# SyncE takes over the stores of the result, GpSimd copies the zero-padded half of v on chip, and the order of the steps is replaced

## The chip, the cores and the metric

The kernel runs on one core of one Trainium2 chip. The core has five engines with a queue each: TensorE (PE, with its weight loads PEld), VectorE (DVE), ScalarE (ACT), GpSimd (POOL) and SyncE (SP, which here only issues transfers). The metric is the device time of one execution in microseconds (us); lower is better. The kernel before took 326.9 us (median of three runs, 325.95 to 327.83).

## The reference

The inputs q, k, v, a_re and a_im have 4 batches, 8 heads, 768 steps and 48 columns. For each batch and head a complex state of 48x48 decays from step to step and takes in the outer product of k and v; q reads its real part:

```python
scale = np.minimum(mag, 0.999) / (mag + 1e-06)      # mag = |a|, a = a_re + i a_im
for t in range(S):
    S_re, S_im = ar*S_re - ai*S_im + kv, ar*S_im + ai*S_re
    y[:, :, t] = einsum('bhd,bhde->bhe', q[:, :, t], S_re)
```

The heads of a step are then laid side by side as x (768 rows of 384 columns for each batch). A causal convolution over five steps, column by column, goes through a sigmoid and gives a gate; x @ w_val is multiplied by the gate, and the product by w_out is the result:

```python
gate = 1.0 / (1.0 + np.exp(-gate_pre))
return (gate * (x @ w_val) @ w_out)
```

## The kernel before, in words

**Attention.** The decay is a product of complex numbers, so the kernel takes its logarithm (level) and its angle, sums both up along the steps, and scales k by the inverse of the running product (giving `kx`) and q by the product itself (`qx`). Real and imaginary part lie side by side, 96 columns for a head. Work is cut into nine units (`UNITS`): of batch 0 the first half of the steps in two units of 2 and 6 heads, and then each half of the steps of a batch with all 8 heads. For a unit ScalarE and VectorE compute the scaled q and k (letters `a` to `r` of the order). TensorE transposes them (`T`, line 524), ScalarE copies each transposed tile out of PSUM (`U`, line 532 by the helper at line 150): 128 such copies in all. `kx` also goes to DRAM and back (`K` and `N`), because the state needs it with the steps on the partitions.

A half of the steps has three chunks of 128 steps; with pairs of head rows this gives 51 chunks. For each chunk TensorE makes the scores (`s`), VectorE multiplies them by a triangular mask (`M`), TensorE adds k and v into the state (`t`), ScalarE copies the state out (`u`), TensorE makes the outputs (`y`, lines 626 to 637) and ScalarE copies them out (`v`, into `y_sb`).

**The padded half of v.** A chunk's scores are packed into three blocks of 64 columns, and the first of them belongs to one head on partitions 0 to 63 and to its partner head on partitions 64 to 127. The matmul at line 637 therefore takes its weights from `v_lo`: a copy of v's first 64 steps of each chunk, at partitions 0 to 63 for heads 0 to 3 and at 64 to 127 for heads 4 to 7, with zeros elsewhere. `v_lo` is one buffer for all batches, cleared once (line 278). `load_vl` fills it by two DMAs per unit from DRAM, ten in all, right after the loads of v (`V`); for the next batch they must wait until the last output of the batch before has read it.

**Convolution and projection.** The finished outputs are moved into `xT`, with columns on the partitions, by small DMAs (`X`, 80 issues, on GpSimd's queue). VectorE and ScalarE compute the convolution (`C`, `D`) and the sigmoid (`G`). TensorE multiplies by w_val (`P`, line 719, 24 steps of six matmul instructions) and by w_out (`O`, line 726, 24 steps of six); VectorE multiplies by the gate (`Z`); ScalarE copies a projected block of 128 rows out of PSUM (`Q`) into `ot`, which has two buffers, and the block is stored (`W`, 24 DMAs).

**The guard.** `guard` (`E`, three steps) checks on VectorE that the sums stayed in range, adds up the hits on TensorE (line 507) and writes one integer, `flag` (line 509). After the last step every engine loads the flag (line 821) and branches around a slow fallback (line 937), which is not taken here. Then the program ends with each engine's drain and a barrier among the engines (line 963).

**What sets the order.** `ORDER` is a string of 1119 letters. Each letter runs one step of its stream (`streams`, line 804), and each engine's instructions keep the order in which the steps issue them: `turn` ties every instruction of TensorE, VectorE and ScalarE to the one before. With `PIN_SP = False` the instructions of SyncE and GpSimd are not tied so and the framework places them. `dma` takes its queue from the stream's letter: those in `POOLQ` go to GpSimd's queue, the others to SyncE's. So in the kernel before GpSimd issues `X` and `W`, and SyncE all the loads and `K`.

ScalarE needs another table when it changes between the function sets of `a`, `c`, `f`, `p` (logarithm and exponential), of `o` (sine; `d` may use either this or the next) and of `G` (sigmoid); the order of the steps fixes how many table loads there are.

Of the kernel before, what the change touches and what calls it, by code (L numbers as in the profile page):

```python
# [10 lines left out]
F32 = mybir.dt.float32  # L11
# [16 lines left out]
PIN_SP = False  # L28
POOLQ = 'XW'
TAP0 = 'act'  # L30
ORDER = (
    "AaaabaLwwwwwwAbwwVAcccefgiilmceAAAdhhjdphhkkLjkkqAfgiinproAoqrKnooaalmppNwwbcdcqrTTAATqraKVthehUafuj"
    "bktUcTTUgkceUUisMsiuslnfMdtgwoioThNyilmpUTUmAATUhqMLTTvUUTUTuUpyvTTtqUTsMyutssrTTpuMUUvryUMUtwsvyTpT"
    "AuAaMwvabtTwssUuwcyMvjAkceAktKNyMvTUUUuryvtTfTgwqnUAAAATTiyUUssTTTXMutivoyoqusUTdtUUUlTuUUtTMTXXTXvy"
    "rmXutMaKhThvyaUTUbUsvwMjpXkcUqyvsMcsMkUpTuUNyvTTynVUUvTTeXrXwwXUUsstwTMTTMTsXfgywooutvMyutqCvCyCDDCu"
    "DtUUTUUATUTTTUUUsUvuwTsTPUMysTMCCdthGvuDhUPUDjGArZtyZTaMTTvyaiUUKkNUvTTiUluknssUbcmpCTTPMUyCtCswdMMu"
    "tvTooyAqAPAuCAXUvyqGZOTcQZTteOpUTAUutTrrUTQOvhUTuUXfsgiMisaabyUUvlKsXTTcMyhmjXUcMvykNkWQXpXPPZVvetpn"
    "oToXWqZOUTODDDDutUTUCTCutXQTCUTUsTDsUPCutMDDdsyGCUPMGZDTDWhWQDAZqhvryuvOQGPZrfWWtugAOOUjMQUaakQATUTA"
    "yTUbUTTUTUiUvcissWlMyTkncsUTTUmMvtuKpNATMUqUyvWoPTZTTyUUAeoTTvTsMtufsyMsqKNgtivypuAitUOUTMUTUXrXTvyd"
    "QuthUhjvTuUPUkUssMsyvMlknooWmZPZpyvOQprOQMyvVtuqTUTUTTUUtTrTTUUUTTUTTTUsMUsyTTMqrXXutvuyvtustUUUUuMX"  # L40
    "XTTTXCXKyTUTUssUMMWvyNTsTvyMDUUUDCUtvyuTTTvCUCTTUUstUUsMWTCsMyMutTDTTCCGXDXUTvyutXUTUvyutXUUUssMsMPP"
    "vyMPPZDvyXCOvuXCCyGZPQGZZZWODvXXCDDDPZDGDCQWDDDPDZPCOQWOQOOWQQOECCGZPCDPGDDPZCCOCCCCCCCWQOWQGWOZPQDD"
    "GZGZOWQOOWEEWQWQQWW"
# [9 lines left out]
def kernel(  # L53
# [140 lines left out]
    def load_vl(u):  # L194
        b, h0, g, f0, nf = units[u]
        for w in range(2):
            hs = slice(w * (H // 2) + h0, w * (H // 2) + h0 + g // 2)
            dma(
                "V", out=v_lo[w * HC:(w + 1) * HC, hs].rearrange("i h n e -> i (h n) e"),
                in_=v[b, hs].rearrange("h (n w i) e -> w i (h n) e", w=2, i=HC)[0],  # L200
            )
# [75 lines left out]
    v_lo = const.tile([C, H, NCH, D], F32, name="v_lo")  # L277
    nc.gpsimd.memset(v_lo, 0.0)
# [513 lines left out]
    def v_loads():  # L792
        for u, (b, h0, g, f0, nf) in enumerate(units):
            if f0 == 0:
                load_v(u)
                load_vl(u)
                yield
# [170 lines left out]
```

## Time and profile before

| | us |
|---|---|
| median of three runs | 326.9 |
| profiled execution | 327.57 |
| its span on the core | 325.9 |
| PE busy | 279.0 |
| ACT busy | 241.3 |
| DVE busy | 240.1 |
| POOL busy | 59.6 |

The span goes from the first to the last instruction of one execution; the profiled execution's own time is 1.7 us longer. An engine's busy time is the union of its instructions. Matmuls overlap one another and their ends are modelled, so a busy PE need not be working at its peak. Issuing, waiting, loading the flag and branching are sequencer work (shown as PEq, SPq and so on) and do not count as busy. A row that names a waiting instruction, an arrow and a releaser says what ended the wait, how long the waits were in total, how many there were and the longest of them.

### The profile page before, as it was taken

To read this page: it belongs to the slowest core of one execution; us is meant where nothing else is said; L and a number is where in the kernel's file an instruction comes from. 1 tells how busy PE (TensorE), PEld (TensorE's weight loads), DVE (VectorE), ACT (ScalarE), POOL (GpSimd) and SP (SyncE) were. 2 spreads that over 40 slices of the span, in tenths; PEclk is the share of its full clock that TensorE was granted. 3 is DMA by queue.
4 is the path that set the end of the run, shared out by engine and by line. 5 is a ranking of instruction groups with operands and counts; after the bars stand their busy time and mean duration, and the time that the engine had idled before them with its cause. 6 is when DMAs were issued, how large, how long until landed. Compare 5 with 4: busy or idle time off the path is not lost.

```text
span 325.9 us, 7175 instructions
## 1 busy us (share of the span) xinstructions
PE 279.0 (86%) x2887; PEld 209.5 (64%) x2887; DVE 240.1 (74%) x289; ACT 241.3 (74%) x430; POOL 59.6 (18%) x129
## 2 busy tenths in 40 slices
PE   0341578999998999999999999999999999999960
PEld 0220356888778778677776778777888966555530
DVE  6798899999999899897799956765637436646500
ACT  5999999999998999989985998858477604114310
POOL 6000000032330302033000223304033120321110
PEclk9999999999999999999999999999999999999995
DMA  7997999899999999779994981734555010121120
GB/s 187 270 224 186 296 279 334 266 256 245 253 207 253 314 213 208 241 229 250 183 160 163 277 204 38 261 91 100 110 188 129 3 36 24 39 76 68 71 80 6
DMA packets 84278, 57.18 MB, mean 175 GB/s; under 512 B 40959, under 2 KB 80142, under 8 KB 83342
## 3 DMA queue, kind: packets, MB, share of 16 engines
q1 hardware_dynamic: 80142, 47.21, 59.8%
q0 software_dynamic: 4096, 9.44, 10.7%
q8 instruction: 25, 0.41, 0.6%
q14 instruction: 15, 0.12, 0.1%
HBM read 37.76 MB, written 14.16 MB: 159 GB/s over the span
## 4 chain that ended last, share of the span: by engine, by line
PE 51%; ACT 17%; issue 11%; DMA 9%; DVE 4%; POOL 3%; SPq 1%; POOLq 0%; ACTq 0%
PE mm L719 10%; PE mm L524 8%; PE mm L726 7%; PE S_ps L591 6%; PE y_ps L626 5%; PE sc_ps L553 5%; DMA v_lo<-in_v_dram 4%; ACT tmp L147 4%; PE mm L361 2%; PE y_ps L636 2%; PE y_ps L631 2%; ACT lv L147 2%; ACT kT L150 2%; POOL out_dram L157 2%; PE sc_ps L555 2%
## 5 line engine op out<-in xcount | busy, mean ns | idle before, releaser
L157 POOL DMA_DIRECT2D xT<-y_sb x80 | 41.0, 519 | 72.5 <-ACT y_sb L150 72.3
L688 DVE SCALAR_TENSOR_TENSOR z<-xT,cw_sb,z 128x768 f32<-128x768 f32 (+1 forms) x60 | 50.2, 854 | 5.2 <-ACT z L147 4.3
L719 PE MATMUL mm<-xT,w_sb 128*128 128x384 f32 x144 | 50.2, 493 | 0.0
L726 PE MATMUL mm<-w_sb,z 128*128 128x384 f32 x144 | 49.6, 491 | 0.0
L569 DVE TENSOR_TENSOR sm<-sc_ps,mask 128x384 f32<-128x384 f32 (+1 forms) x51 | 26.8, 530 | 29.4 <-PE sc_ps L558 21.2
L591 PE MATMUL S_ps<-v_in,kn 128*96 128x48 f32 x320 | 35.6, 252 | 7.4 <-DMA kn<-kd 6.2
L591 PEld LDWEIGHTS S_ps<-v_in,kn 128*96 128x96 f32 x320 | 32.4, 168 | 13.4 <-DMA kn<-kd 6.0
L150 ACT COPY y_sb<-y_ps 112x256 f32<-112x256 f32 (+1 forms) x51 | 19.0, 373 | 29.1 <-PE y_ps L636 29.1
L726 PEld LDWEIGHTS mm<-w_sb,z 128*128 128x128 f32 x144 | 26.5, 190 | 17.0 <-ACT kT L150 0.5
L553 PE MATMUL sc_ps<-qT,kT 96*64 96x128 f32 x192 | 36.6, 287 | 0.6 <-DVE sm L569 0.6
L554 PE MATMUL sc_ps<-qT,kT 96*64 96x128 f32 x192 | 36.7, 287 | 0.5 <-ACT qT L150 0.5
L719 PEld LDWEIGHTS mm<-xT,w_sb 128*128 128x128 f32 x144 | 26.4, 190 | 16.6
L145 ACT ACT_TABLE_LOAD x25 | 32.1, 1283 | 1.2 <-PEq L952 0.8
L157 POOL DMA_DIRECT2D out_dram<-ot x24 | 13.2, 550 | 104.4 <-ACT ot L150 86.8
L524 PE MATMUL mm<-ident,kx 128*96 128x128 f32 x192 | 30.0, 286 | 1.5 <-DVE lv L441 0.7
L150 ACT COPY kT<-mm 96x384 f32<-96x384 f32 x64 | 28.6, 486 | 0.5 <-PE sc_ps L558 0.2
L150 ACT COPY ot<-mm 128x384 f32<-128x384 f32 x24 | 11.4, 474 | 23.6 <-PE mm L726 13.1
L150 ACT COPY qT<-mm 96x384 f32<-96x384 f32 x64 | 28.2, 492 | 0.8 <-PE mm L524 0.7
L524 PE MATMUL mm<-ident,qx 128*96 128x128 f32 x192 | 28.3, 280 | 0.2 <-DVE cw_sb L331 0.2
L555 PE MATMUL sc_ps<-qT,kT 96*64 96x64 f32 x192 | 27.3, 224 | 0.0
L558 PE MATMUL sc_ps<-qT,kT 96*64 96x64 f32 x192 | 27.1, 223 | 0.0
L743 DVE TENSOR_TENSOR z<-mm,z 128x384 f32<-128x384 f32 x24 | 13.0, 554 | 15.6 <-ACT z L147 9.4
(90 smaller groups left out, 586.5 us busy)
## 6 DMA issues: line engine op xcount, KB each, us to landing
kd<-kx SPq DMA_DIRECT2D x7, 1152.0 KB, 5.6
out_dram<-ot POOLq DMA_DIRECT2D x24, 192.0 KB, 2.2
ar_in<-in_a_re_dram SPq DMA_DIRECT2D x7, 576.0 KB, 8.9
ai_in<-in_a_im_dram SPq DMA_DIRECT2D x7, 576.0 KB, 9.7
k_in<-in_k_dram SPq DMA_DIRECT2D x7, 576.0 KB, 6.5
q_in<-in_q_dram SPq DMA_DIRECT2D x7, 576.0 KB, 7.8
kn<-kd SPq DMA_DIRECT2D x7, 576.0 KB, 4.4
kn<-kd SPq DMA_DIRECT2D x14, 288.0 KB, 6.3
```

Of the source, the lines that this page charges most:

```text
L145: turn("act", nc.scalar.preload_act_table_set(sets[0]))
L150: return turn("act", nc.scalar.copy(out, in_))
L157: ins = (nc.gpsimd if pool else nc.sync).dma_start(**kw)
L524: pe(nc.tensor.transpose(pt[:C2, j, :], src[:, j, f, h, :], ident))
L553: pe(nc.tensor.matmul(lo[:, :C], part(u, 0, ha, n, 0, HC), part(u, 1, ha, n), start=True, stop=True))
L554: pe(nc.tensor.matmul(hi[:, 0::2], part(u, 0, hb, n, 0, HC), qb, start=True, stop=True))
L555: pe(nc.tensor.matmul(lo[:, C:], part(u, 0, hb, n, HC, C), part(u, 1, hb, n, HC, C), start=True, stop=True))
L558: pe(nc.tensor.matmul(hi[:, 1], part(u, 0, ha, n, HC, C), part(u, 1, ha, n, HC, C), start=True, stop=True))
L591: pe(nc.tensor.matmul(S_ps[bank(u, rs)][:C2, (2 * (h0 + r) + w) * D:(2 * (h0 + r) + w + 1) * D], kn[:, at:at + C2], v_b[b][:, head(u, h), ...
L688: dve(nc.vector.scalar_tensor_tensor(out=z, in0=xT[:, c, EXT + t0 - t:EXT + t0 - t + n], scalar=cw_sb[:, TAPS - 1 - t, c:c + 1], in1=z, op ...
L719: pe(nc.tensor.matmul(pv[:, :n], wv_sb[:, ci, c * P:(c + 1) * P], xT[:, ci, EXT + t0:EXT + t0 + n], start=(ci == 0), stop=(ci == NT - 1),))
L726: pe(nc.tensor.matmul(po[:, :DM], z[:, ci, m:m + P], wo_sb[:, ci, :], start=(ci == 0), stop=(ci == NT - 1)))
```

## The change

Five edits. `POOLQ` loses `W`, so SyncE issues the 24 stores of the result. `PIN_SP` is true, so SyncE's and GpSimd's instructions keep the order of the steps too. `load_vl` and its ten DMAs go; a new stream `B`, with one step per unit, copies the same part of v from `v_in` to `v_lo` on GpSimd, two copies per unit. `v_lo` is now two buffers, one for each half of the steps. `ORDER` is a new string of 1128 letters, in which the guard's steps stand further ahead of the end.

```diff
--- before.py
+++ after.py
@@ -25,22 +25,22 @@
 GROUPWISE = True
 BUFS = {'in': 4, 'v': 2, 'kn': 2, 'xT': 2, 'z': 2, 'lv': 2, 'an': 2, 'tmp': 2, 'qx': 2, 'kx': 1, 'kT': 6, 'S': 1, 'S_sb': 3, 'S_cr': 4, 'y_sb': 3, 'sm': 2, 'ot': 2, 'mm': 4, 'y': 1}
 XSTEP = 2
-PIN_SP = False
-POOLQ = 'XW'
+PIN_SP = True
+POOLQ = 'X'
 TAP0 = 'act'
 ORDER = (
-    "AaaabaLwwwwwwAbwwVAcccefgiilmceAAAdhhjdphhkkLjkkqAfgiinproAoqrKnooaalmppNwwbcdcqrTTAATqraKVthehUafuj"
-    "bktUcTTUgkceUUisMsiuslnfMdtgwoioThNyilmpUTUmAATUhqMLTTvUUTUTuUpyvTTtqUTsMyutssrTTpuMUUvryUMUtwsvyTpT"
-    "AuAaMwvabtTwssUuwcyMvjAkceAktKNyMvTUUUuryvtTfTgwqnUAAAATTiyUUssTTTXMutivoyoqusUTdtUUUlTuUUtTMTXXTXvy"
-    "rmXutMaKhThvyaUTUbUsvwMjpXkcUqyvsMcsMkUpTuUNyvTTynVUUvTTeXrXwwXUUsstwTMTTMTsXfgywooutvMyutqCvCyCDDCu"
-    "DtUUTUUATUTTTUUUsUvuwTsTPUMysTMCCdthGvuDhUPUDjGArZtyZTaMTTvyaiUUKkNUvTTiUluknssUbcmpCTTPMUyCtCswdMMu"
-    "tvTooyAqAPAuCAXUvyqGZOTcQZTteOpUTAUutTrrUTQOvhUTuUXfsgiMisaabyUUvlKsXTTcMyhmjXUcMvykNkWQXpXPPZVvetpn"
-    "oToXWqZOUTODDDDutUTUCTCutXQTCUTUsTDsUPCutMDDdsyGCUPMGZDTDWhWQDAZqhvryuvOQGPZrfWWtugAOOUjMQUaakQATUTA"
-    "yTUbUTTUTUiUvcissWlMyTkncsUTTUmMvtuKpNATMUqUyvWoPTZTTyUUAeoTTvTsMtufsyMsqKNgtivypuAitUOUTMUTUXrXTvyd"
-    "QuthUhjvTuUPUkUssMsyvMlknooWmZPZpyvOQprOQMyvVtuqTUTUTTUUtTrTTUUUTTUTTTUsMUsyTTMqrXXutvuyvtustUUUUuMX"
-    "XTTTXCXKyTUTUssUMMWvyNTsTvyMDUUUDCUtvyuTTTvCUCTTUUstUUsMWTCsMyMutTDTTCCGXDXUTvyutXUTUvyutXUUUssMsMPP"
-    "vyMPPZDvyXCOvuXCCyGZPQGZZZWODvXXCDDDPZDGDCQWDDDPDZPCOQWOQOOWQQOECCGZPCDPGDDPZCCOCCCCCCCWQOWQGWOZPQDD"
-    "GZGZOWQOOWEEWQWQQWW"
+    "AAVLaaAbcceafgadiibclmhhdcwjwwwhhjwkknpewpBfkkwwoVgqArowqriinooTTBAaAaUAlmpbUpTUqATUrKcdqTUTLwssANtr"
+    "TaTTuAhMMyhacUjwUUbsvceyvkcMskseBfnKtugfMigTdiyvtuilwooilshympAAANtmvMuTThqUUqtujUUtuprMTrUTTtyTuVUU"
+    "UTTTvysMpkUtvTpsMkUsTautaUyuAbUMTvTKUAqUAcywTTvyNcUUsesUMMsrvTntfXXyoouwvgUTMdTtyUUXvTTiUXutqBUAhATr"
+    "AhiATwauyUwLUalmpjtsskTTpTvMMbUUsUywcMvkTTcUUwTUyvTXTunTewyUTTqUsTUUwvosoMsyrMwMXvXKNtuATTUfUyvqgBUX"
+    "UrPituTXCDDTTtyUUKUuNasMstTTaUiulvDsUyCmXCMTCMtCvCCDPputypGZCUDACvuPtdhTTuhtUTUTCGybUUssjutPvkwXMysk"
+    "wPGcuZZZdhtTMMnovoyTUTTZAAqOcrvyqhQXeUTTUTUTUTXXUTUUUTjvUsfAAsrMyaMsvkayMPukvyVOnboBvgcWZKUoNiilmXXX"
+    "DXtDuTDCCCOUtQDWTTTDQTAAutUTUUUssDDUcOMWDDupTpMOOrtQTWQTyCCqGWUvsAQDuydMvTUUtuUTTTAAtUqKrhPhGGPyeaUU"
+    "sTvjNaZTUMyfubZcgBkPPPkZviiltZXZVmssMydnooTAXpTMTutvyBchqWUTUTUTUTeUUUUTTTUfqOKsspMgMiivysvyhutQUUTr"
+    "TTvUMTUlmuAyUUvssMyMrvpsMyvTTjUTTpUUUXXNtuXXkkTTTUtUunPZotuTTqTyBUUUssMMTToTvysvyqUUArrKNUUtuTUTTtuO"
+    "vQXMyUUsvsMyMvsMyvTTtuTTUUUtuUTTtUTTTutUyUUssUXvCDMyvMsyCXCCuvTUMTTCCUUTUtWWPTTTUCyuCUUssXMMvyvCDDDD"
+    "CsMyEPvOOQQXWWXOQWGZXXPPPGZGZZZPtODCOOuCDDDDDCCQWDDDDCZQWQWyGvXOQWPZGEEGOQWOQWOCQPPZDCZOOCCCGDQDDDWG"
+    "QWXCCPZPPCCCGOZZOOOQWQWWQQWW"
 )
 TURN = 2.0 ** 24
 RADIAN = 2.0 * PI / 2.0 ** 32 * (1.0 - 2.0 ** -22)
@@ -191,14 +191,15 @@
 
 
 
-    def load_vl(u):
+    def early(u):
         b, h0, g, f0, nf = units[u]
         for w in range(2):
             hs = slice(w * (H // 2) + h0, w * (H // 2) + h0 + g // 2)
-            dma(
-                "V", out=v_lo[w * HC:(w + 1) * HC, hs].rearrange("i h n e -> i (h n) e"),
-                in_=v[b, hs].rearrange("h (n w i) e -> w i (h n) e", w=2, i=HC)[0],
-            )
+            pool(nc.gpsimd.tensor_copy(
+                out=v_lo[f0][w * HC:(w + 1) * HC, hs],
+                in_=v_b[b][w * HC:(w + 1) * HC, hs, f0 * HN:(f0 + nf) * HN],
+            ))
+        yield
 
     def load_kn(u, f):
         b, h0, g, f0, nf = units[u]
@@ -274,8 +275,9 @@
     wv_sb, wo_sb = w_sb
     cw_sb = const.tile([P, TAPS, NT], F32, name="cw_sb")
 
-    v_lo = const.tile([C, H, NCH, D], F32, name="v_lo")
-    nc.gpsimd.memset(v_lo, 0.0)
+    v_lo = [const.tile([C, H, HN, D], F32, name=f"v_lo{i}") for i in range(2)]
+    for t in v_lo:
+        nc.gpsimd.memset(t, 0.0)
 
     y_ps = [ps.tile([P, 512], F32, name=f"y_ps{i}") for i in range(BUFS["y"])]
     sc_ps = [ps.tile([P, 512], F32, name=f"sc_ps{i}") for i in range(2)]
@@ -634,7 +636,8 @@
                 ))
             for r, w, h in heads:
                 pe(nc.tensor.matmul(
-                    to(r, w, 0, HC), v_lo[:, head(u, h), n], sm[:, r, :HC], start=False, stop=True, skip_group_check=True
+                    to(r, w, 0, HC), v_lo[n // HN][:, head(u, h), n % HN], sm[:, r, :HC],
+                    start=False, stop=True, skip_group_check=True,
                 ))
             yield
 
@@ -793,7 +796,6 @@
         for u, (b, h0, g, f0, nf) in enumerate(units):
             if f0 == 0:
                 load_v(u)
-                load_vl(u)
                 yield
 
     def kd_stores():
@@ -802,7 +804,7 @@
             yield
 
     streams = {
-        "A": loads(), "V": v_loads(), "N": halves(load_kn),
+        "A": loads(), "V": v_loads(), "B": each(early), "N": halves(load_kn),
         "K": kd_stores(), "L": raw_loads(), "w": weights(),
         "a": each(p_ln), "b": each(p_tan), "c": each(p_sec), "d": each(p_arc), "e": each(p_mag), "f": each(p_inv),
         "g": each(p_min), "h": each(p_add("an")), "i": each(p_add("lv")), "j": each(p_off(1)), "k": each(p_turn),
```

## Rows read from the trace of the kernel before

**Rows 1.** The page's first part: busy us (share of the span) xinstructions.

```profile
PE 279.0 (86%) x2887; PEld 209.5 (64%) x2887; DVE 240.1 (74%) x289; ACT 241.3 (74%) x430; POOL 59.6 (18%) x129
```

**Rows 2.** Stretches (us): length, busy PE, PEld, DVE, ACT, POOL, PEclk, DMA share, GB/s.

```profile
25.00:50.00 25.00, 12.77 (x65) 8.32 (x65) 22.51 (x24) 24.63 (x31) 0.00 (x0) 1.00 0.98 259
25.00:125.00 100.00, 83.84 (x1047) 67.77 (x1048) 95.35 (x100) 97.86 (x171) 15.75 (x32) 1.00 1.07 257
150.00:200.00 50.00, 50.00 (x485) 37.07 (x485) 39.47 (x44) 42.02 (x71) 10.56 (x21) 1.00 0.81 189
125.00:300.00 175.00, 174.16 (x1777) 129.78 (x1776) 119.84 (x144) 118.35 (x220) 35.58 (x70) 1.00 0.55 140
300.00:326.00 26.00, 14.62 (x47) 8.28 (x46) 5.93 (x11) 4.23 (x9) 3.25 (x6) 0.82 0.14 49
```

**Rows 3.** Timeline by engine, last output step and end: start, us, engine, line, operation.

```profile
275.21 0.39 PE L636 MATMUL y_ps<-sm,v_lo 128*48 128x64 f32 x8
...
308.54 5.97 PE L726 MATMUL mm<-w_sb,z 128*128 128x384 f32 x18
...
314.58 0.48 ACT L150 COPY ot<-mm 128x384 f32<-128x384 f32 x1 [1.46 <-PE mm L726]
...
315.36 0.54 POOL L157 DMA_DIRECT2D out_dram<-ot  x1 [1.39 <-ACT ot L150]
...
146.77 0.37 SPq L157 DMA_DIRECT2D ai_in<-in_a_im_dram  x1
```

**Rows 4.** Sequencer rows of lines 821, 937, 963: min/median/max ns, first and last start.

```profile
L821 SPq TENSOR_LOAD <-flag x1: 483/483/483, 314.8 to 314.8; - x1
L821 POOLq TENSOR_LOAD <-flag x1: 499/499/499, 315.3 to 315.3; - x1
L937 PEldq COMPARE_BRANCH  x1: 4402/4402/4402, 315.5 to 315.5; - x1
L963 POOLq EVENT_SEMAPHORE  x4: 17/17/17, 325.1 to 325.8; - x4
L963 POOLq DRAIN  x3: 44/107/8559, 316.5 to 325.6; - x3
L963 SPq DRAIN  x3: 7/7/13, 320.4 to 325.3; - x3
```

**Rows 5.** Waits of PE and SP by releaser: us in total, times, longest.

```profile
PE y_ps L636 <- DMA v_lo<-in_v_dram: 1.4, 2, 0.9
...
SPq L157 <- PE y_ps L636: 19.7, 2, 15.7
```

**Rows 6.** Groups by shape, ACT: count, busy us, mean ns, idle before.

```profile
L145 ACT ACT_TABLE_LOAD x25 | 32.1, 1283 | 1.2 <-PEq L952 0.8
L150 ACT COPY kT<-mm 96x384 f32<-96x384 f32 x64 | 28.6, 486 | 0.5 <-PE sc_ps L558 0.2 <-PE mm L524 0.2
...
L147 ACT ACTIVATE an<-lv 128x1152 f32<-128x1152 f32 x7 | 8.2, 1169 | 0.1
```

**Rows 7.** Groups by shape, GpSimd and VectorE.

```profile
L278 POOL MEMSET v_lo<- 128x2304 f32 x1 | 2.0, 2012 | 0.0
...
L267 POOL MEMSET b_quart<- 128x1 f32 x1 | 0.1, 93 | 0.0
...
L433 DVE TENSOR_SCALAR an<-an 128x1152 uint32<-128x1152 uint32 x7 | 5.3, 752 | 0.0
```

**Rows 8.** Timeline of the start, DVE and POOL; then the mask copies' own row.

```profile
2.35 2.58 DVE L253 TENSOR_SCALAR dturn<-dmat 128x256 f32<-128x256 f32 x1 [2.35 <-POOL dmat L248]
...
2.78 2.01 POOL L278 MEMSET v_lo<- 128x2304 f32 x1
...
L265 POOL COPY mask<-tri x4: 229/238/282, 4.7 to 5.4; 64x64 f32<-64x64 f32 x4
```

**Rows 9.** DMA issues: queue, operation, count, KB each, median us to landing.

```profile
out_dram<-ot POOLq DMA_DIRECT2D x24, 192.0 KB, 2.2
ar_in<-in_a_re_dram SPq DMA_DIRECT2D x7, 576.0 KB, 8.9
```

## The prediction

> **What bounds the kernel now.** I first read the page's busy times and then the stretches. PE is the busiest engine, 279.0 of 325.9 us [rows 1]. From 125 to 300 us it is busy for 174.2 of 175 us, while DVE and ACT have a third of that time free [rows 2]. Between 25 and 125 us it is another kernel: ACT 97.9%, DVE 95.4%, PE only 83.8%, and in 25 to 50 us PE has only 12.8 of 25 us [rows 2]. There PE lacks work because ScalarE and VectorE are still making the scaled q and k. So there are three stretches: a supply-bound one to about 125 us, a PE-bound one to the last matmul, and an end. The end is the third view. The last projection matmul finishes at 308.54 + 5.97 = 314.5 us, the last copy to `ot` at 314.58 + 0.48 = 315.06, and the last store is issued at 315.36 [rows 3]. Yet the span lasts to 325.9. That is 11.4 us behind the last matmul, in which nothing is computed.
>
> **The end, term 1.** The rows of lines 821 to 963 say what these 11.4 us are. SyncE loads the flag at 314.8 and reaches its drain at 320.4; PE branches at 315.5 for 4.4 us, to 319.9. GpSimd begins a drain of 8.56 us at about 316.5, so it ends at 325.1, and the final barrier begins then [rows 4]. SyncE has waited 4.7 us for GpSimd by that time. The drain follows GpSimd's flag load at 315.3, which waits for `flag`, and GpSimd's last store at 315.36 [rows 3, 4]. Two edits together free it. With `W` on SyncE, GpSimd's last transfers are the `X` of the last unit. With the guard ahead, the flag is not made behind the last projection: in the new string the guard's matmul has 14 `P` and `O` steps behind it (5 and 9). One takes PE about 1.94 us (5.97 for three, less the overlap of the ends) [rows 3]. That is 27 us, so the flag is there at about 288. The last `y` step has 16 such steps behind it (20 before), 31 us; its copy and `X` issues take a few us more, so GpSimd goes idle near 290, and an 8.56 us drain ends near 300, covered by projections. If only one edit acted, the cover would be gone: a flag made last keeps GpSimd's drain beginning near 316, and the gain falls to below 1 us.
>
> Late next is SyncE. It begins its last store at 315.06 + 0.3 (the gap GpSimd's store shows), issues in 0.37 us (SyncE's own row) and then loads the flag at 315.7 instead of 314.8 [rows 3, 4]. From flag load to drain it took 320.4 - 314.8 = 5.6 us, and from GpSimd's event to the end of the span 325.9 - 325.1 = 0.8 us [rows 4]. That gives 315.7 + 5.6 + 0.8 = 322.1 against 325.9: **-3.8 us**. The store's own landing (2.2 us after issue [rows 9], so 317.9) is hidden beneath. Bounds: if SyncE too were shorter, PE's branch (4.4 us behind a flag load some 0.9 us earlier, so to 319.0) plus 0.8 would end at 319.8, -6.1. If GpSimd's drain in fact runs on from the last store's landing at 317.9, the end is 317.9 + 8.6 + 0.8 = 327.3, +1.4. I take -3.8, since SyncE's rows are measured.
>
> **v's padded half, term 2.** Ten DMAs go. PE waited for them 1.4 us in two waits, and SyncE stood 19.7 us (once 15.7) until PE's outputs had let go of `v_lo` [rows 5]. PE's waits end: **-1.4 us**. The SyncE waits cost nothing I can find at PE apart from these, so they count zero; at worst (for the good) SyncE's earlier loads give another 1 us.
>
> In their place come 18 GpSimd copies, two for each unit: 144 elements a partition for unit 0, 432 for unit 1 and 576 for the others, 9216 in all, of which 4608 belong to units 0 to 4, whose copies stand in the first 125 us or so. No row shows such a copy. The long memset gives (2.012 - 0.093)/2303 = 0.83 ns an element, which makes 0.57 us of 576 elements; the 64x64 mask copies give (0.238 - 0.093)/64 = 2.3 ns, which makes 1.40 us [rows 7, 8]. The ten early copies thus take GpSimd 4.8 to 11.4 us. GpSimd has the time: 15.8 of 100 us busy there [rows 2]. `B` stands 67 to 135 letters of the string ahead of the outputs that read it, at 0.29 us a letter (326/1128) some 20 us or more, so PE should not wait for it. What can cost is VectorE. At the start a VectorE scaling of 256 columns lasted 2.58 us, until 4.93, beside a GpSimd memset that ran from 2.78 to 4.79; the same kind of operation over 1152 columns otherwise takes 0.75 us [rows 7, 8]. If the early copies hold VectorE for their length, it loses 4.8 to 11.4 us in a stretch where it has 4.65 us free [rows 2]: 0 to 6.7 us on the path. I take 0.75 us a copy, between the row that is long and the row that is a copy, 6.2 us in all: **+1.5 us**.
>
> The Trainium skill, SBUF — State Buffer, section "Who interferes with whom", says that a VectorE instruction with two SBUF inputs contends with a GpSimd instruction that reads SBUF, and that the second to issue is blocked for the whole of the other. By that rule the copies, unlike a memset, would hold back nearly every VectorE operation of this stretch; the trace agrees as far as the one long scaling goes, and the sum would then be at the upper end, +6.7 instead of +1.5.
>
> **The order, term 3.** I counted from the two strings how much ScalarE work stands ahead of the same step, with each step at its row's mean less 0.1 us of overlap (0.39 a transposed copy, 1.07 an activation of a full unit) and 1.28 for each table load [rows 6]. Ahead of the 8th of the 128 transposed copies stand 46.2 us before and 33.6 now; of the 16th 53.2 and 52.7; of the 32nd 80.0 and 78.8; of the 64th 134.5 and 132.3; of the 96th 193.7 and 191.2. Table loads go from 25 to 24. So the first heads come sooner, and the supply then runs about 1 us ahead. I take the value at the 32nd, inside the supply-bound stretch: **-1.2 us**. Bounds by the same count: the 41st copy is 9 us ahead and the 57th 10 us behind, so if half of such a lead or lag is kept, -4.5 to +5.
>
> **Moves at zero.** The stores leave GpSimd 24 issues of 0.55 us lighter, which nothing waits for. `v_lo` in two buffers lets the first half of a batch be copied while the second half is still read. SyncE's loads, now pinned between stores, keep waiting as they did.
>
> **Sum.** -3.8 - 1.4 + 1.5 - 1.2 = -4.9. The profiled execution took 327.57 us, so 322.7; it lies 0.7 above the median of 326.9, against which the forecast is 322.0.
>
> **Rivals.**
> *A, the forecast:* 322.0, own range 318.5 to 325.2. Chance 0.46.
> *B, the drain stays last:* GpSimd's drain may depend on something other than its own last work, such as the last store's landing. For: no row shows it in any other place. Against: SyncE's drains take nanoseconds [rows 4]. Without term 1: 325.8; no change. Chance 0.14.
> *C, PE's early gap fills:* the 12.6 us by which the first eight copies come sooner fall where PE has 12.2 us free [rows 2]; if a third of that is used and kept, 4 us more go: 318. Against: by the 16th copy the lead is 0.5 us. Chance 0.21.
> *D, slower: the copies hold VectorE up.* Place: 25 to 125 us; price up to 1.40 us a copy, 11.4 us for ten. If VectorE's free time is not where the copies are, all of it is on the path: 322.0 - 1.5 + 11.4 = 332. It decides from 7.9 us on the path (328.5). Against: GpSimd must also win its turn each time. Chance 0.13.
> *E, stores behind loads:* a store took 2.2 us to land from GpSimd's queue, a 576 KB load from SyncE's 8.9 [rows 9]. In SyncE's queue a store behind such a load would free `ot` 6.7 us later; ScalarE comes back to that buffer two projections (3.9 us) later and would stand 2.8 us. Six stores lie among loads, in two runs: 5.6 us if ScalarE's 8 free us between 150 and 200 [rows 2] do not absorb it: 327.6, no change. Chance 0.06.
>
> The Trainium skill, DMA: Bandwidth & Descriptors, section "Queues, rings and completion order", says that a DMA engine takes turns between queues but works through one ring in order. That speaks against moving the stores; only the different landing times above bear on it, and no row here shows a store on SyncE's queue.
>
> **How the numbers follow.** A measurement of this kernel can tell about 0.5% from no change, so faster means below 325.3 and slower above 328.5. Faster: A and C, 0.67. Same: B and E, 0.20. Slower: D, 0.13. The range of 315.5 to 329.5 holds A, B, E, nearly all of C and the milder part of D; some 0.13 is left out.
>
> **What would show it.** Right: GpSimd's long drain begins before 305 and ends before SyncE's; the span ends about 7.5 us behind the last matmul instead of 11.4; no PE wait on `v_lo`. Copies of about 0.75 us, with VectorE operations beside them longer than their rows here, would show term 2; a longer 25 to 125 us stretch would show D; ScalarE waits on `ot` for a DMA would show E. The forecast is wrong if the last matmul ends more than 3 us from 313.4, or if something else holds the end.

## The result, and the profile after

The changed kernel takes 320.38 us (median of 4 runs, 316.98 to 322.99), the kernel before 327.37 us in the same session. The ratio is 0.971, with a 95% interval of 0.966 to 0.976: 2.9% faster. The forecast was 322.0. Two of the four runs took 317.0 and 317.9 us and two 322.8 and 323.0; here and below a median is over all runs and a ratio over the faster group alone.

The profile taken with the result is of the 322.99 us execution. The rows below are of a second run of the same kernel (profiled at 318.41 us, span 316.62), and that is set against before's 327.57 us (span 325.88). Line numbers have moved by 2 or 3: 821 is now 823, 937 is 939, 963 is 965.

The difference of 9.16 us splits at the last projection matmul. It ended at 314.50 and now ends at 310.53: 3.97 us, the *body*. From there to the end of the span it was 11.37 us and is 6.09: 5.28 us, the *tail*. The time outside of the span (1.69 and 1.79) gives 0.1 back. The forecast had 1.1 for the body and 3.8 for the tail. The body's gain is not in every execution: in the first profile the last projection matmul ended at 315.40, with a tail of 5.80.

First the page's busy row of PE (columns as in [rows 1]), then the stretches that answer to [rows 2]:

```profile
PE 275.4 (87%) x2887; PEld 211.5 (67%) x2887; DVE 240.0 (76%) x289; ACT 239.2 (76%) x429; POOL 62.4 (20%) x124
```

```profile
25.00:50.00 25.00, 15.60 (x124) 11.00 (x124) 24.44 (x28) 24.89 (x36) 1.14 (x2) 0.86 1.17 284
25.00:125.00 100.00, 85.74 (x1060) 70.07 (x1061) 96.61 (x101) 97.32 (x173) 15.52 (x25) 0.95 0.92 238
125.00:300.00 175.00, 171.80 (x1777) 131.24 (x1776) 122.81 (x148) 117.42 (x219) 36.26 (x71) 0.99 0.56 141
```

Between 25 and 50 us PE is busy for 15.6 us instead of 12.77 [rows 2], so it does find more to do early. But look at the clock column: 0.86 there, where it was 1.00. The changed kernel has stretches in which TensorE is granted half its clock (1.2 instead of 2.4 GHz): 6.8 us from 42.8, 3.4 from 73.5 and 3.4 from 237.4. Before had none ahead of its last matmul.

Where the body's 4 us came from can't be read from PE's idle time: up to its last projection matmul PE was idle for 314.5 - 279.0 = 35.5 us and is now for 310.5 - 275.4 = 35.1. So I took from the trace the time from each matmul's start to the next one's, and subtracted the full-clock median of its kind of step (323 ns for a projection, 85 for `S_ps`, 47 for `sc_ps`, and so on; a kind is what a matmul writes and its first operand, and the medians are over the profiles compared). What is left over, in us, is an estimate that moves by some us with how finely the kinds are cut; a gap counts as short when the time from start to start is up to 1 us:

```
                         gaps up to 1 us   gaps over 1 us   at half clock
before                        27.1              22.9             0.0
changed, second run           17.3              23.4             5.9
```

The new order takes 9.8 us out of short gaps, which the page counts mostly as busy. A little over half of that lies where PE changes from one kind of step to another, the rest between matmuls of one kind. The mean from start to start where PE leaves `sc_ps` for another kind of step was 143 ns and is 80 (at full clock); where it leaves `y_ps<-sm`, 174 and 124. 5.9 of the 9.8 us are given back at half clock and 0.5 in long gaps. That leaves 3.4 of the 4.0.

The tail. Sequencer rows as in [rows 4]:

```profile
L823 SPq TENSOR_LOAD <-flag x1: 477/477/477, 283.9 to 283.9; - x1
L823 POOLq TENSOR_LOAD <-flag x1: 498/498/498, 283.9 to 283.9; - x1
...
L939 SPq EVENT_SEMAPHORE  x8: 17/17/17, 314.4 to 314.9; - x8
...
L939 PEldq COMPARE_BRANCH  x1: 4222/4222/4222, 305.2 to 305.2; - x1
...
L939 SPq COMPARE_BRANCH  x1: 45/45/45, 311.7 to 311.7; - x1
...
L965 POOLq DRAIN  x3: 38/107/6594, 285.0 to 316.4; - x3
L965 SPq DRAIN  x3: 7/7/13, 315.7 to 316.1; - x3
```

GpSimd's long drain begins at 285.0 and lasts 6.59 us, so it is over at 291.6, 25 us ahead of the end; it was 8.56 us from 316.5 [rows 4]. SyncE holds the end now: its last store is issued by 311.7, it branches there, its eight events follow at 314.4, and the span ends at 316.6. Its flag load stands at 283.9, *ahead* of the stores.

The end in the timeline (columns as in [rows 3]; brackets give the idle time ahead and what ended it), and then the stores' landing, which answers to [rows 9]:

```profile
302.63 7.90 PE L729 MATMUL mm<-w_sb,z 128*128 128x384 f32 x24
...
305.31 6.37 SPq L157 DMA_DIRECT2D out_dram<-ot  x4
...
310.61 0.48 ACT L150 COPY ot<-mm 128x384 f32<-128x384 f32 x1 [0.64 <-PE mm L729]
```

```profile
out_dram<-ot SPq DMA_DIRECT2D x24, 192.0 KB, 2.0
ar_in<-in_a_re_dram SPq DMA_DIRECT2D x7, 576.0 KB, 7.2
```

The copies as one group, with what GpSimd waited for ahead of them, and then PE's four largest waits (us in total, times, longest):

```profile
L198 POOL COPY v_lo<-v_in 64x576 f32<-64x576 f32 (+2 forms) x18 | 15.8, 877 | 44.5 <-PE y_ps L638 33.3 <-DMA v_in<-in_v_dram 7.4 <-PE mm L526 3.2
```

```profile
PE mm L363 <- DVE lv L353: 10.4, 4, 8.3
PE mm L526 <- DVE kx L477: 8.1, 2, 5.8
PE S_ps L593 <- DMA kn<-kd: 5.1, 2, 2.9
PE mm L331 <- DVE cw_row L325: 3.1, 1, 3.1
```

No PE wait on `v_lo` is left (1.4 us in [rows 5]), but PE waits 18.5 us for VectorE's `lv` and `kx`: the long gaps have changed places, not gone.

### The profile page after: what moved, and what is told of

Its sections match the earlier page's. It is cut to its first block, busy times and chain, and to the rows that moved or that the text cites. A ratio compares the mean times of both kernels' runs of the same rounds, so it can differ in the third digit from the quotient of the medians.

```text
span 321.2 us, 7175 instructions
## 1 busy us (share of the span) xinstructions
PE 280.0 (87%) x2887; PEld 215.7 (67%) x2887; DVE 240.0 (75%) x289; ACT 239.3 (74%) x429; POOL 62.5 (19%) x124
## 4 chain that ended last, share of the span: by engine, by line
PE 61%; ACT 19%; DMA 7%; DVE 7%; issue 2%; SPq 1%; POOL 0%; ACTq 0%; DVEq 0%; POOLq 0%
PE mm L729 14%; PE mm L722 14%; PE mm L526 8%; PE S_ps L593 6%; DMA kn<-kd 5%; PE y_ps L628 5%; ACT L145 4%; PE sc_ps L555 4%; ACT tmp L147 4%; ACT qx L147 3%; PE y_ps L633 3%; PE y_ps L638 2%; ACT an L147 2%; ACT lv L147 2%; PE mm L363 2%
## 5 line engine op out<-in xcount | busy, mean ns | idle before, releaser
L593 PEld LDWEIGHTS S_ps<-v_in,kn 128*96 128x96 f32 x320 | 34.2, 174 | 12.1 <-issue 7.1
L729 PEld LDWEIGHTS mm<-w_sb,z 128*128 128x128 f32 x144 | 26.6, 190 | 16.8
L556 PE MATMUL sc_ps<-qT,kT 96*64 96x128 f32 x192 | 37.8, 293 | 0.0
L555 PE MATMUL sc_ps<-qT,kT 96*64 96x128 f32 x192 | 37.3, 291 | 0.1
L526 PEld LDWEIGHTS mm<-ident,kx 128*96 128x96 f32 x192 | 21.9, 137 | 11.4 <-issue 9.1
L526 PE MATMUL mm<-ident,qx 128*96 128x128 f32 x192 | 28.7, 289 | 0.5 <-DVE lv L443 0.5
L557 PE MATMUL sc_ps<-qT,kT 96*64 96x64 f32 x192 | 27.8, 228 | 0.0
L560 PE MATMUL sc_ps<-qT,kT 96*64 96x64 f32 x192 | 27.7, 227 | 0.0
L746 DVE TENSOR_TENSOR z<-mm,z 128x384 f32<-128x384 f32 x24 | 13.0, 553 | 18.5 <-PE mm L722 12.4
```

The source lines that it names most:

```text
L526: pe(nc.tensor.transpose(pt[:C2, j, :], src[:, j, f, h, :], ident))
L555: pe(nc.tensor.matmul(lo[:, :C], part(u, 0, ha, n, 0, HC), part(u, 1, ha, n), start=True, stop=True))
L556: pe(nc.tensor.matmul(hi[:, 0::2], part(u, 0, hb, n, 0, HC), qb, start=True, stop=True))
L557: pe(nc.tensor.matmul(lo[:, C:], part(u, 0, hb, n, HC, C), part(u, 1, hb, n, HC, C), start=True, stop=True))
L593: pe(nc.tensor.matmul(S_ps[bank(u, rs)][:C2, (2 * (h0 + r) + w) * D:(2 * (h0 + r) + w + 1) * D], kn[:, at:at + C2], v_b[b][:, head(u, h), ...
L729: pe(nc.tensor.matmul(po[:, :DM], z[:, ci, m:m + P], wo_sb[:, ci, :], start=(ci == 0), stop=(ci == NT - 1)))
```

## The experiments

Each was timed in 3 rounds (the last store on ScalarE in 5) beside the kernel before. "Last matmul" is the end of the last projection matmul in the profiled execution.

```
kernel                                us      ratio to before [95%]   last matmul  tail
changed, again                      317.93    0.972 [0.965, 0.979]       310.53    6.09
stores back on GpSimd               332.56    1.011 [1.006, 1.017]       319.97   11.06
flag made last                      322.28    0.986 [0.978, 0.993]       311.51    8.90
before + both edits of the end      322.75    0.984 [0.981, 0.988]       314.78    5.90
the same + copies                   323.39    0.987 [0.979, 0.995]       316.07    5.78
copies made twice                   327.95    not settled                318.02    5.80
padded half by DMA, 1 buffer        354.79    1.083 [1.074, 1.092]       345.6     6.39
padded half by DMA, 2 buffers       331.56    1.016 [1.010, 1.023]       324.17    5.07
one memset                          318.35    0.971 [0.964, 0.979]       309.34    6.38
new order, not pinned               327.11    0.994 [0.990, 0.997]       319.45    6.03
before, X on SyncE                  323.80    0.989 [0.985, 0.994]       315.06    6.71
last store on ScalarE               318.96    0.968 [0.963, 0.972]       314.08    4.50
```

### The changed kernel again

> The kernel after, unchanged, for a second profile. Theory (the end became shorter and the rest hardly moved): 317 to 323 us; from the last matmul to the end of the span 5.8 us, GpSimd's drain 6.6 us long and over before the last store. Rival (the body became shorter as well): with TensorE granted full speed from 45 us to the end, the last matmul ends near 310 us, some 4 us ahead of the kernel before.

Measured: 317.93 us (317.15 to 321.34). The result stands; the rows of this run are those shown above.

### The end: stores, flag, or both

The changed kernel with the stores back on GpSimd:

```diff
-POOLQ = 'X'
+POOLQ = 'XW'
```

> The kernel after, but GpSimd issues the 24 stores again; order, copies and early flag stay. Theory (the drain starts behind GpSimd's last transfer and lasts 82 ns for each transfer that GpSimd issued: 8559 ns for 104 before, 6594 ns for 80 after): drain 8.6 us, last again, 11.3 us from the last matmul to the end, 5.5 us slower than after. Rival (the early flag alone does it): no slower than after by more than 1 us.

The changed kernel with the guard's two `E` steps moved behind the last `O`:

```diff
-"...yGvXOQWPZGEEGOQWOQW...OOOQWQWWQQWW"
+"...yGvXOQWPZGGOQWOQW...OOOEEQWQWWQQWW"
```

> The kernel after, but the guard's matmul and the flag stand behind the last projection, as in the kernel before; SyncE keeps the stores. Theory (GpSimd's drain waits for the flag and lasts 82 ns for each of 80 transfers): drain begins 2 us behind the last matmul, lasts 6.6 us, 0.8 us more to the end: 9.4 us of end, 3.6 us slower than after. Rival (the drain follows the last store or the last transfer only): as after within 1 us.

The kernel before with only those two edits (in its own order):

```diff
-POOLQ = 'XW'
+POOLQ = 'X'
-"...QOECCGZ...OOWEEWQWQQWW"
+"...QOEEECCGZ...OOWWQWQQWW"
```

> The kernel before with its order, its DMAs for v's padded half and SyncE and GpSimd not pinned, but SyncE issues the stores and the guard's matmul and flag follow right behind the guard's first step (10 projection steps ahead of the end). Theory (the end alone): 5.8 us from the last matmul to the end instead of 11.4, so 5.6 us faster than before, about 321.5 us. Rival (the stores stand behind loads in SyncE's queue and hold ScalarE up): the last matmul ends 2 us or more later than before and the gain is under 4 us.

The drain row of GpSimd with the flag made last (before with both edits has the same 6594 ns, from 296.3):

```profile
L965 POOLq DRAIN  x3: 38/107/6594, 313.0 to 320.1; - x3
```

With the flag last, the 6.59 us drain runs from 313.0 to 319.6 and is again the last thing: 0.8 us later the span ends. The tail is 8.90, 2.8 more than in the changed kernel. With the stores on GpSimd and the flag early, the drain starts at 321.65, lasts 8.56 us again, and the tail is 11.06. So of the 5.3 us of tail the stores alone bring 2.5 (2.0 of it a shorter drain), the flag alone 0.3, and the two together the rest. Both in the old order give the whole tail (5.90) at an unchanged body (314.78 against 314.50): 1.6% without a new order or a copy.

The stores on GpSimd also cost the *body* 9.4 us (319.97 against 310.53), which I had not expected. PE runs its matmuls in the same order in both kernels, so they can be compared one by one: this kernel is 2.3 us behind the changed one at 150 us and 9.4 behind at 160. The waits of that kernel between 140 and 170 us, and its chain from 151 us (start, us, what):

```profile
ACT z L147 <- DMA xT<-y_sb: 4.5, 1, 4.5
PE S_ps L593 <- ACT S_sb L150: 3.9, 1, 3.9
```

```profile
151.81 0.97 POOL xT L157 x2
152.78 6.51 DMA xT<-y_sb
...
159.39 0.30 ACT S_sb L150
...
159.74 1.51 PE S_ps L593 x8
```

The transposing DMAs issued at 151.8 landed at 159.3, ScalarE waited there with `S_sb` queued behind its `z`, and PE waited for `S_sb`. They were not issued late: the changed kernel issues the same ones at 149.5, 2.3 us sooner, which is the lag that was there already. They took longer: between 140 and 165 us the median from issue to landing is 5.4 us, and 2.2 in the changed kernel. The loads of the next batch on SyncE's queue are the difference beside them, here and then in the changed kernel:

```profile
145.75 0.60 SPq L157 DMA_DIRECT2D k_in<-in_k_dram  x1
146.40 1.16 SPq L157 DMA_DIRECT2D q_in<-in_q_dram  x1
```

```profile
154.83 0.43 SPq L157 DMA_DIRECT2D k_in<-in_k_dram  x1
155.31 0.68 SPq L157 DMA_DIRECT2D q_in<-in_q_dram  x1
```

With the stores gone from its queue, SyncE no longer stands at them and sends these loads 9 us sooner, into the time of the transposing DMAs. That the loads are what made the DMAs slower is the likely reading; no run holds back the loads alone.

### What the drain's length hangs on

The kernel before, with `X` on SyncE and only the 24 stores left on GpSimd:

```diff
-POOLQ = 'XW'
+POOLQ = 'W'
```

> The kernel before, with the X transposing DMAs issued by SyncE and only the stores of the result left on GpSimd; flag and order as before. Theory 1: GpSimd's closing drain grows with the number of DMAs that GpSimd has issued, 82.3 ns each (8559 ns with 104, 6594 ns with 80): with 24 it takes 1.98 us, begins near 316.5 as before, and no longer ends last; SyncE and PE then hold the end and the tail is 6 to 8 us instead of 11.4. Theory 2: the drain has a fixed part or follows the landing of the last store: it stays above 5 us, tail 9 to 11.4 us. The body can change by some us either way, since X moves to SyncE's queue behind its loads: theory 1 gives 321 to 327 in all, theory 2 325 to 331.

```profile
L963 POOLq DRAIN  x3: 40/107/4222, 316.7 to 321.5; - x3
```

The drain is 4.22 us with 24 DMAs, against 6.59 with the 80 `X` and 8.56 with all 104. It shrinks with the DMAs that GpSimd has issued, but theory 1's 82.3 ns each, which fits 80 and 104, would make 1.98: it falls as a law. Three points fit a fixed 2.26 us with 54 ns an `X` and 82 ns a store, but three terms always fit three points, so that stays open. What is shown is that the landing of the last transfer doesn't set it: with the flag made last it is 6594 ns though the last `X` had been issued some 30 us earlier. The tail fell to 6.71 although the drain still ends last (316.72 + 4.22 = 320.94, the end at 321.76).

### The copies

Before with both edits of the end, and besides the copies and two buffers at nine `B` in the old order:

```diff
 # load_vl's two DMAs a batch half become, for each unit:
+pool(nc.gpsimd.tensor_copy(out=v_lo[f0][...], in_=v_b[b][...]))   # twice
```

> b_both and, in place of the ten DMAs of v's padded half, the GpSimd copies with two buffers; the order is still that of the kernel before, with nine B steps put in, and SyncE and GpSimd are not pinned. It asks where the 4 us come from by which the last matmul of the kernel after ends sooner than that of b_both (310.5 against 314.8 us). Theory (the new order with its pins): the last matmul stays within 1 us of 314.8, time 322 to 323.5 us. Rival 1 (the copies, by the DMA time and the waits they take away): 2 us or more sooner, 320.5 us or less. Rival 2 (the start: with v_lo cleared in two parts VectorE's first scaling no longer lasts until 4.9 us): 2 us sooner as well, and seen already at the first transposed copies.

323.39 against 322.75 us without the copies, with overlapping intervals. PE's waits on `v_lo` (1.8 us there) are gone, VectorE's busy time goes from 237.9 to 240.5, and the last matmul comes 1.3 us later. Waits saved and VectorE held come out about even; in the old order the copies bring no gain of their own.

How a copy and VectorE meet shows in the timeline of the changed kernel:

```profile
66.69 1.35 DVE L399 SCALAR_TENSOR_TENSOR lv<-lv,tmp 128x1152 f32<-128x1152 f32 x1
```

```profile
66.79 2.50 POOL L198 COPY v_lo<-v_in 64x576 f32<-64x576 f32 x2 [6.67 <-PE y_ps L638]
```

```profile
94.86 1.82 DVE L316 SCALAR_TENSOR_TENSOR w_sb<-raw,cvt 128x1152 f32<-128x1152 uint32 x1
```

The first copy at 66.79 begins 0.1 us behind a VectorE operation that runs to 68.04, and lasts until 68.57: 1.78 us, where copies with no VectorE operation beside them take 0.66. At 94.86 it is the other way round: a copy has run since 94.38 and ends at 95.47, and VectorE's operation takes 1.82 us where the same one takes 1.35 at 65.42. So either engine can be the one that stands, and mostly it was GpSimd: its fourteen copies of 576 took 3.9 us more in all than at 0.66 each.

Each copy made twice in the changed kernel:

```diff
+            pool(nc.gpsimd.tensor_copy(out=v_lo[f0][...], in_=v_b[b][...]))   # again, same operands
```

> The kernel after, but each GpSimd copy of v's half is made twice. Theory (where a copy and VectorE meet, GpSimd waits: copies of 576 elements took 0.67 us alone and up to 1.8 us beside VectorE, and VectorE's own operations grew by about 2 us in all): at most 1 us slower. Rival D of the prediction (the copies hold VectorE up): 18 more copies, 10 of them in the stretch to 125 us where VectorE is busy for 96%, 6 us or more slower.

The last matmul comes 7.5 us later. I had allowed 1 us. By the same matmul it is 0.6 us behind the changed kernel at 100 us and 6.8 at 120. The place is GpSimd's queue, shown in the timeline of its instructions, and the waits of that kernel from 95 to 112 us:

```profile
94.95 2.83 POOL L198 COPY v_lo<-v_in 64x576 f32<-64x576 f32 x2 [4.81 <-PE y_ps L644]
97.83 3.41 POOL L204 COPY v_lo<-v_in 64x576 f32<-64x576 f32 x2
101.19 3.95 POOL L157 DMA_DIRECT2D xT<-y_sb  x8
```

```profile
ACT z L147 <- DMA xT<-y_sb: 3.0, 1, 3.0
...
PE sc_ps L561 <- ACT qT L150: 2.8, 1, 2.8
DVE z L697 <- ACT z L147: 2.2, 1, 2.2
```

In the changed kernel the eight `X` follow the first pair at 97.15; here at 101.19. ScalarE's `z` waits for the DMA, PE for ScalarE, and PE then runs at half clock from 111.7 for 6.8 us. VectorE's busy time rose by only 4.7 us (240.0 to 244.7).

The padded half by DMA again in the new order. The first try kept one buffer and before's two DMAs at each `V`:

> The kernel after with its order, pins, stores on SyncE and early flag, but v's padded half is loaded by DMAs again, right behind v, into one buffer. Theory (the new order gives the 4 us): up to 2 us slower than after, for the waits at SyncE until the outputs have let go of the buffer. Rival (the copies give them): 4 us slower or more, with PE waits on v_lo.

That kernel loads the next batch's half before the last outputs of the batch before have read the old one, so part of `y` is computed from other data. It took 354.79 us with SyncE standing 88 us at stores; nothing on the copies follows from it. The second try loads at the copies' places, into two buffers, and computes the whole result:

```diff
-            pool(nc.gpsimd.tensor_copy(out=v_lo[f0][...], in_=v_b[b][...]))
+            for n in range(HN):
+                s0 = (f0 * HN + n) * C
+                dma("V", out=v_lo[f0][w * HC:(w + 1) * HC, hs, n],
+                    in_=v[b, hs, s0:s0 + HC].rearrange("h i e -> i h e"))
```

> The changed kernel with the padded half of v brought by DMAs again, at the places where the on-chip copies stand (six small DMAs a step on SyncE's queue in place of two GpSimd copies), two buffers, order and pins unchanged. It computes the whole result. Theory 1: the copies cost VectorE and GpSimd's queue about 1.5 us before 125 us and nothing later: without them VectorE's busy time falls by 1 to 4 us and the last matmul comes 0 to 2 us sooner, 308.5 to 310.5, if SyncE's 108 more issues are hidden; time 316 to 319. Theory 2: what matters is SyncE's queue: SyncE stands at the places where the copies waited for PE (33 us in the changed kernel), later loads and stores stand behind it, and the last matmul comes 3 us or more later, time 321 or more.

331.56 us: theory 2. VectorE's busy time falls by 1.6 us (240.0 to 238.4), as theory 1 had it, and yet the last matmul comes 13.6 us later. SyncE's queue, early on:

```profile
31.53 5.33 SPq L157 DMA_DIRECT2D v_lo<-in_v_dram  x6
36.96 0.68 SPq L157 DMA_DIRECT2D kd<-kx  x1
```

The copies' nine steps became 54 DMAs (not 108, as expected). `kd<-kx` of the second unit goes out at 36.96 instead of 30.3, and later ones fall back further (147.8 instead of 137.3). In the pinned order, then, it pays to have the padded half off SyncE's queue. With six small DMAs a unit this overstates what before's larger ones would cost.

### The start

One buffer tile and one memset of 2304 columns, as before had it:

```diff
-    v_lo = [const.tile([C, H, HN, D], F32, name=f"v_lo{i}") for i in range(2)]
-    for t in v_lo:
-        nc.gpsimd.memset(t, 0.0)
+    v_lo_all = const.tile([C, 2, H, HN, D], F32, name="v_lo")
+    nc.gpsimd.memset(v_lo_all, 0.0)
+    v_lo = [v_lo_all[:, i] for i in range(2)]
```

> The kernel after, but v_lo is one tile of which the two halves are parts, so that it is cleared by one memset of 2304 columns as before, not by two with the mask copies between. Theory (the start carries through): VectorE's first scaling ends near 4.9 us instead of 2.9, the first transposed copy comes 2 us later, and so does the end: 320 us. Rival (ScalarE makes it up): the first copies come later, the last matmul does not, time as after within 1 us.

318.35 us: no difference. The start of that kernel, VectorE's scaling and then GpSimd's memset:

```profile
2.34 0.56 DVE L254 TENSOR_SCALAR dturn<-dmat 128x256 f32<-128x256 f32 x1 [2.34 <-POOL dmat L249]
```

```profile
2.76 2.11 POOL L279 MEMSET v_lo<- 128x2304 f32 x1
```

The scaling takes 0.56 us here beside the long memset; before with both edits shows 0.56 too, with before's memset unchanged. But the 2.58 us of [rows 8] is no accident of one execution. With the flag made last the same two rows are:

```profile
2.35 1.62 DVE L254 TENSOR_SCALAR dturn<-dmat 128x256 f32<-128x256 f32 x1 [2.35 <-POOL dmat L249]
```

```profile
2.78 1.05 POOL L280 MEMSET v_lo<- 128x1152 f32 x1
```

Four of the fourteen profiles have it (before 2.58; flag made last, stores on GpSimd and last store on ScalarE 1.62), and in each the scaling ends some 0.15 us behind the memset: at 4.93 and 4.79 us with 2304 columns, at 3.97 and 3.83 with 1152. In the other ten it takes 0.56, and the two small memsets just ahead of the long one take 0.21 to 0.24 us each instead of 0.09. So the scaling either lasts until the memset is over or is out of its way, and one kernel can do either: before with both edits starts as before does and shows 0.56. This run fell on the side where it is out of the way, so its profile does not show what the other side costs with the long memset. With 1152 columns it cost about 1 us: the three new-order profiles that have it are 1.1 to 1.2 us behind the changed kernel at 25 us, and with the flag made last it is still 1.2 at 200 us.

### The order, and the pins

The changed kernel with `PIN_SP = False`:

```diff
-PIN_SP = True
+PIN_SP = False
```

> The changed kernel with its new order, but SyncE and GpSimd no longer held to the written order: each of their instructions is placed by the planner as before the change. Theory 1: the 4 us gained in the body come from the order of PE, ScalarE and VectorE work; the pins are worth nothing: last projection matmul at 309 to 312, time 316.5 to 320. Theory 2: the gain needs SyncE's loads and GpSimd's copies at their written places: last matmul 313 to 317, time 320 to 324.

327.11 us, the last matmul at 319.45: worse than either theory. By the measure above the short gaps are 17.3 us, just as with the pins, so that gain belongs to the order of PE, ScalarE and VectorE work. But long gaps rise from 23.4 to 28.7 and half clock from 5.9 to 10.0. Its chain of waits across 137 to 156 us, then that of 125 to 175 us as stretches:

```profile
137.86 7.22 DMA kd<-kx
...
145.15 0.37 SPq L157
...
145.58 7.61 DMA kn<-kd
153.19 1.42 issue
154.61 1.17 PE S_ps L593 x6
```

```profile
125.00:150.00 25.00, 25.00 (x291) 18.74 (x289) 24.31 (x27) 23.80 (x36) 10.57 (x22) 1.00 0.75 223
150.00:175.00 25.00, 21.87 (x179) 16.08 (x178) 16.81 (x19) 18.49 (x32) 2.18 (x5) 0.86 0.75 154
```

`kx` goes out to DRAM and comes back transposed as `kn`. With the pins the first `kn` is issued at 142.2, here at 145.2: it waits for `kd<-kx` and comes 7.3 us behind it instead of 4.9. Then the `kn` DMAs took 6.7 to 8.3 us to land instead of 4.4 to 6.0, so that the data are there at 153.2, PE stands, and half clock follows. Here too SyncE's loads of the next batch went out sooner: `k_in` and `q_in` at 133.7 and 135.0 instead of 154.8 and 155.3. By the same matmul this kernel is 0.6 us behind the changed one at 150 us and 6.9 at 155. Over 150 to 175 us PE is busy for 21.87 us, against 25.00 in the changed kernel. The last matmul ends at 314.8 in the old order without pins, at 319.5 in the new order without, at 310.5 in the new order with them. The new order gains only as long as SyncE's queue follows it. The old order with pins was not run, so it is not shown what the pins alone would bring.

### A version that might beat both

The changed kernel, the very last store issued by ScalarE:

```diff
-            dma("W", out=out[b, t0 + m:t0 + m + P], in_=ots.pop(0))
+            if (b, t0, m) == rows[-1]:
+                turn("act", nc.scalar.dma_start(out=out[b, t0 + m:t0 + m + P], in_=ots.pop(0)))
+            else:
+                dma("W", out=out[b, t0 + m:t0 + m + P], in_=ots.pop(0))
```

> The changed kernel, but the very last store of the result is issued by ScalarE, the engine that made the last copy to ot, so that SyncE's last store is the one before. Theory 1: in the changed kernel the end is held by SyncE, whose branch over the guarded block begins 0.33 us after the last store is issued and takes 2.6 to 3 us; with the last store taken away from it, SyncE branches about 2 us sooner, the end is then held by PE's branch or the landing of the store, and the tail behind the last projection matmul falls from 5.8 to 6.1 us to 4 to 5 us; time 316 to 317.5. Theory 2: the end hangs on the landing of the last store and on the closing barrier, and ScalarE's own issue and branch take SyncE's place: tail 5.7 to 6.2 us, time as the changed kernel's, 318 to 320.

Columns as in [rows 4]:

```profile
L942 SPq EVENT_SEMAPHORE  x8: 17/17/17, 316.4 to 316.9; - x8
...
L942 SPq COMPARE_BRANCH  x1: 45/45/45, 313.5 to 313.5; - x1
L942 PEldq EVENT_SEMAPHORE  x1: 51/51/51, 314.1 to 314.1; - x1
...
L942 ACTq EVENT_SEMAPHORE  x1: 17/17/17, 316.1 to 316.1; - x1
```

SyncE branches 0.6 us ahead of the end of the last matmul (314.08), and the tail is 4.50 us, 1.3 to 1.6 less than in the two profiles of the changed kernel, as theory 1 had it. SyncE's events are still the last to come, 0.3 us behind ScalarE's. In time, 318.96 us and a ratio of 0.968 [0.963, 0.972] can't be told from the changed kernel's 0.972 [0.965, 0.979]. Theory 1's 316 to 317.5 us is not reached. Its profile has 17.0 us at half clock ahead of the end (6.8 from 45.9, 6.8 from 76.7, 3.4 from 240.5) where the changed kernel's has 13.6, VectorE's scaling at the start took 1.62 us, and the last matmul comes 3.6 us later with the same body: a gain of some 1.5 us in the tail drowns in that.

## Why the prediction was right or wrong

The forecast of 322.0 lies close to the median of 320.4, but that is partly luck: between the two profiles compared the drop was 9.2 us where the sum had 4.9, with both the end and the body gaining more than forecast. The last matmul, at 310.5, is 2.9 us from the forecast's 313.4, just inside the 3 us that it allowed.

**The end, term 1: right in mechanism, 5.3 us instead of 3.8.** Both edits are needed, the drain starts at 285 ("GpSimd goes idle near 290"), and SyncE is late next. The step that was mis-sized is "then loads the flag at 315.7": I placed the flag load behind the last store. With the flag early, it had run at 283.9, and SyncE branched straight behind the store, so the tail was 6.1 and not 7.5. "If only one edit acted ... the gain falls to below 1 us" holds for the flag alone (0.3), not for the stores alone (2.5), since I had taken the drain's 8.56 us for fixed; it was 6.59 with 80 DMAs.

**v's padded half, term 2: even, as summed (-1.4 + 1.5), by a different division.** The waits on `v_lo` went. A copy of 576 took 0.94 us where I took 0.75; 18 copies made 15.8 us of GpSimd. VectorE's busy time rose by 1.6 to 2.6 us in the two comparisons with and without copies, where I had charged 6.2 us of holding for the early ten. The memset's 2.58 us row, on which the range's upper end rested, is a real meeting of the two engines, but it says how long VectorE stands when it comes off worse, not how often it does; beside the copies it was mostly GpSimd that stood. The rule of the Trainium skill, SBUF — State Buffer, section "Who interferes with whom", that the second to issue is blocked for the whole of the other, agrees with the two meetings shown above (a copy of 1.78 us behind VectorE, a VectorE operation of 1.82 us behind a copy). What the forecast drew from it, that nearly every VectorE operation would be held back, did not come: that took GpSimd to be always first.

**The order, term 3: right in sign, too small, and counted on the wrong thing.** I counted ScalarE's work ahead of the n-th transposed copy and took the lead at the 32nd, 1.2 us. The trace has that copy end at 84.2 instead of 85.2 us, the 41st 9.3 us ahead and the 57th 9.4 behind (9 and 10 by the count), so the count of ScalarE's work was sound there. But PE's gain of 9.8 us lies in short gaps all along the span (5.9 of it between 200 and 300 us, where I had PE down as full), and the cost of 5.9 us lies in the clock. A count of ScalarE's work holds neither.

**"SyncE's loads, now pinned between stores, keep waiting as they did"** was the step that failed outright: costed at nothing, it decides the sign. In the changed kernel SyncE stands at stores (16.8 us in two waits between 140 and 165 us) and so holds the next batch's loads back, `k_in` until 154.8. Take away the pins or the stores and these loads go out 9 to 21 us sooner, the small DMAs beside them land later (likely for that reason), and the body is 8.9 us later without the pins and 9.4 with the stores on GpSimd. That the waits stayed was the forecast; that the gain hangs on them was not in it.

**Rivals.** B, a drain that stays last: no. C, the early gap filled: in part. 25 to 50 us gained 2.8 us of busy PE, and the last matmul came 4.0 us sooner, near its price, but most of what was gained stands elsewhere. D, the copies hold VectorE up: no, though with the copies doubled its price appeared by another way, through `X` queued behind them. E, stores behind loads: no. The stores landed in 2.0 us (median) from SyncE's queue, 2.2 from GpSimd's, so the turns between queues of the Trainium skill, DMA: Bandwidth & Descriptors, section "Queues, rings and completion order", cost these stores nothing that the trace shows. Two stores did stand 20.6 and 30.1 us in SyncE's queue before they were issued, with no wait of ScalarE behind them. ScalarE waited twice for `ot` (1.6 us until 278.4 and 2.3 until 309.5; before had 0.7), the forecast's sign of E, but both times with PE busy at its projections.

What is not settled is why PE's clock falls. Each of the three stretches at 1.2 GHz begins within some us of an idle PE: 1.5 us from 41.3, 2.1 from 70.2, 2.9 from 233.9. Yet before stood idle for 5.5 us from 24.6 and 4.0 from 31.9 at full clock, and the changed kernel for 5.8 from 24.6, so idle time alone doesn't tell when it comes.

## What to carry to other kernels

Look at what each engine does behind its last useful instruction, and move DMA issues and flags off the engine whose closing work ends last: two small edits gave 1.6% here without touching the body. Judge a new order by the queues that carry it, above all the small DMA round trips: ask which loads run beside them, and what a wait in the loads' queue was holding back. Where PE looks full, measure from start to start of its matmuls and look at its granted clock beside it, since a gain in one can be given back in the other.

## What the hardware showed that I had not expected

- GpSimd's closing drain: 4222 ns with 24 DMAs issued by it, 6594 with 80, 8559 with 104, the same with an early or a late flag.
- PE's jump over the guarded block takes 3.4 to 4.4 us. SyncE's events came 2.4 to 3.1 us behind its own branch in eleven of fourteen profiles and 0.5 in three (stores on GpSimd, padded half by DMA with 2 buffers, before with X on SyncE); ScalarE's came 0.5 behind in all. With the flag early PE's jump lies beneath its last matmuls.
- A VectorE operation of 0.56 us beside a GpSimd memset lasted until the memset's end in four of fourteen profiles (2.58 us with 2304 columns, 1.62 with 1152), and not in the others.
- Transposing DMAs took a median of 5.4 us to land instead of 2.2 in a stretch where two 576 KB loads had gone out 9 us sooner.
